# Value products of two attentions: one head's 64 columns per matmul, both heads in one PSUM bank

## The chip, the cores and the metric

The kernel runs on one core of a Trainium2 chip. TensorE multiplies; VectorE (DVE), ScalarE (ACT) and GpSimd (POOL) work element by element; SyncE (SP) issues most loads. The metric is the device time of one execution in microseconds. Before the change three runs took 876.66, 878.46 and 881.11 us; the median is 878.46.

## What is computed

Two attentions over 4 batches x 8 heads, 576 positions, head width 64, are added, and two MLPs follow on 2304 tokens of width 512:

```python
q_d, k_d, v_d = (a.reshape(B, H, 144, 4, D).mean(axis=3) for a in (q, k, v))   # pooled by 4
out_up = np.repeat(softmax(q_d @ k_d.T / 8) @ v_d, 4, axis=2)
mask = np.abs(pos[:, None] - pos[None, :]) < 4
out_local = softmax(np.where(mask, q @ k.T / 8, -1e9)) @ v
x = tokens(out_up + out_local)                                                  # 2304 x 512
x = np.maximum(np.maximum(x @ w1, x @ w2), x @ w3) @ w_out                      # 512 -> 768 -> 512
return np.maximum(0.01 * (h := x @ w_in), h) @ w_out2                           # 512 -> 2048 -> 512
```

## The kernel before

The tokens are cut into eight units of 288 (half a batch each), and the heads into four pairs; a pair's 2 x 64 values fill 128 rows of a tile.

The local attention of units 0 to 2 runs on TensorE, in steps named by letters: `pl_C` the scores in blocks of 96 queries by 102 keys (64 rows per head, line 399), `pl_D`, `pl_E`, `pl_H` and `pl_I` the softmax, `pl_O` the transposes (line 454), `pl_o` their two copies to `plt` (line 464; the first brings blocks 0 and 1, the second block 2), `pl_P` the value product (line 474), `pl_Q` the sum with the pooled output into `x32` (line 489), `pl_R` and `pl_S` the split of x into a high and a low part. Units 3 to 7 have their local attention as elementwise work on the other engines, called the lanes here: `local_load`, `qk_mult` on GpSimd, `qk_reduce` on VectorE and ScalarE, `pv_mult` and `pv_sum` on VectorE (lines 254 to 308).

The pooled attention of all four batches runs on TensorE: `ds_B` scores (line 548), `ds_M` transposes, `ds_N` the value product over two blocks of 72 keys (line 622), `ds_v` the copy of its output to `up` (lines 635 and 637).

In `pl_P` and `ds_N` before the change the weights are the values of both heads of the pair, 128 columns. Each head's attention is streamed through them, so each product holds 128 rows of which 64 are its head's own; the other 64 are not read. The two heads stand in two PSUM banks (`pl_P`) or in two column ranges of one bank (`ds_N`).

The first MLP layer is line 717 (18 groups of 12 matmuls a unit), its second layer line 747; the second MLP is lines 796 and 820.

Three things set the order. In the start, `ORDER` lists the steps of unit 0 and batch 0 by hand for all engines, with `fill` matmuls (line 169) in between. After it only SP's order is that of the code; for the other engines a scheduler orders the instructions by its own estimates of what is ready when. In both parts every engine works through its list in order. PSUM after the start is split into pools: `mm` with four banks for lines 717, 747 and 474, `at` with two for the pooled attention and transposes, `early` with two for scores.

Of the kernel before, what the change touches and what calls it, by code (L numbers as in the profile page):

```python
# [13 lines left out]
AF = mybir.ActivationFunctionType  # L14
ALU = mybir.AluOpType
# [5 lines left out]
FAC = 4  # L21
SD = S // FAC
# [7 lines left out]
NCOL = G * RU  # L30
# [5 lines left out]
QC = SD // 2  # L36
SCALE = 1.0 / 8.0
MASKED = -8.0e9
QB = 96
KB = QB + 2 * (FAC - 1)  # L40
NBLK = RU * G // QB
# [30 lines left out]
def local_global_attention_moe_kernel(  # L72
# [15 lines left out]
    V, A, P, T = nc.vector, nc.scalar, nc.gpsimd, nc.tensor  # L88
# [19 lines left out]
    for half in range(2):  # L108
        mk = const.tile([128, RC, WIN], F32, name=f"mask{half}")
        P.memset(mk, 0.0)  # L110
        for a in range(4):
            s = mk[32 * a : 32 * a + 32]
            if half == 0:
                P.affine_select(
                    out=s, in_=s, pattern=[[1, RC], [1, WIN]], base=-(FAC - 1),
                    channel_multiplier=1000, compare_op=ALU.is_ge, fill=MASKED,
                )
            else:
                P.affine_select(
                    out=s, in_=s, pattern=[[-1, RC], [-1, WIN]],  # L120
# [21 lines left out]
    for u in range(2):  # L142
# [5 lines left out]
        for j0, n, step, cm, base in conds:  # L148
            P.affine_select(
                out=bd[:, j0 : j0 + n], in_=bd[:, j0 : j0 + n], pattern=[[0, n], [step, KB]], base=base,  # L150
# [4 lines left out]
    def scratch(first, kind, name):  # L155
        if first == 0:
            tag = "l3" if name == "wl3" else "b"
            return PS["0"].tile([128, 512], F32, tag=tag, bufs=6 if tag == "b" else 1, name=name)
        return PS[kind].tile([128, 512], F32, tag=kind, name=name)
# [7 lines left out]
    def fill(what, t, n=None):  # L167
        for _ in range(FILL[what] if n is None else n):
            T.matmul(out=t, lhsT=warm[:, :128], rhs=warm, start=True, stop=True)
# [180 lines left out]
    pl = {}  # L350
# [107 lines left out]
    def pl_o(u, h):  # L458
# [5 lines left out]
            V.tensor_copy(out=t[:, j0:j1], in_=pt)  # L464
        pl[u, h, "aT"] = t

    def pl_P(u, h):
        t = pl.pop((u, h, "aT"))
        ps = pl[u, h, "o"] = [scratch(u, "mm", "ps_lo") for hh in range(2)]
        if u == 0:  # L470
            fill("P", ps[0])
        for hh in range(2):
            for j in range(NBLK):
                T.matmul(  # L474
                    out=ps[hh][:, j * QB : j * QB + QB], lhsT=pl[u // 2, h, "v"][:KB, u % 2, j], rhs=t[:, j, hh],
                    start=True, stop=True,
                )

    def pl_Q(u, h):
        ps = pl.pop((u, h, "o"))  # L480
        if h == 0:
            X[u] = (
                mmp.tile([128, 4, NCOL], F32R, tag="xh", bufs=2, name="xh"),
                mmp.tile([128, 4, NCOL], F32R, tag="xl", bufs=2, name="xl"),
            )
        x32 = pl[u, h, "x32"] = pools[u // 2].tile([128, NCOL], F32, tag="x32", bufs=2, name="x32")
        for hh in range(2):
            rows = slice(64 * hh, 64 * hh + 64)
            V.tensor_tensor(  # L489
                out=x32[rows].rearrange("p (s f) -> p s f", f=FAC),  # L490
                in0=ps[hh][rows, :NCOL].rearrange("p (s f) -> p s f", f=FAC),
                in1=up[u // 2][rows, h, u % 2 * QC : u % 2 * QC + QC].unsqueeze(2).to_broadcast((64, QC, FAC)), op=ALU.add,
            )

    def pl_R(u, h):
        A.activation(out=X[u][0][:, h], in_=pl[u, h, "x32"], func=AF.Copy)
# [7 lines left out]
    up = {}  # L504
    dst = {}
# [109 lines left out]
    def ds_N(b, h):  # L615
        ps = scratch(b, "at", "ps_up")
        if b == 0:
            fill("N", ps)
        ps = dst[b, h, "up"] = ps[:, : 2 * SD].rearrange("p (h s) -> p h s", h=2)
        for hh in range(2):  # L620
            for kc in range(2):
                T.matmul(  # L622
                    out=ps[:, hh], lhsT=dst[b, h, "v"][:, kc].rearrange("p h d -> p (h d)"),
                    rhs=dst[b, h, "aT", kc][:, 2 * hh : 2 * hh + 2].rearrange("p j s -> p (j s)"),
                    start=kc == 0, stop=kc == 1,
                )

    def ds_v(b, h):
        ps = dst.pop((b, h, "up"))
        if h == 0:  # L630
            up[b] = mmp.tile([128, 4, SD], F32, tag="up", bufs=2, name="up")
        for hh in range(2):
            rows = slice(64 * hh, 64 * hh + 64)
            if b == hh == 0:
                V.tensor_copy(out=up[b][rows, h, :], in_=ps[rows, hh])
            else:
                A.activation(out=up[b][rows, h, :], in_=ps[rows, hh], func=AF.Copy)

    def ds_stages(b, h):
        return [  # L640
            lambda: ds_load(b, h, "qk"),
            lambda: ds_pool_qk(b, h),
            lambda: ds_load(b, h, "v"),
            lambda: ds_pool_v(b, h),
            lambda: [f(b, h) for f in (ds_B, ds_F, ds_G, ds_J)],
            lambda: ds_norm(b, h),
            lambda: [f(b, h) for f in (ds_M, ds_m)],
            lambda: [f(b, h) for f in (ds_N, ds_v)],
        ]
# [59 lines left out]
    def L1_mm(u, m, e):  # L709
        xh, xl = X[u]  # L710
        ps = PS['mm'].tile([128, NCOL], F32, tag="mm", name="ps_h")
        terms = ((0, xh), (0, xl), (1, xh))
        order = [(wi, xx, kk) for wi, xx in terms for kk in range(KC)]
        if u == 0:
            order = [(wi, xx, kk) for kk in range(KC) for wi, xx in terms]
        for n, (wi, xx, kk) in enumerate(order):
            T.matmul(  # L717
                out=ps, lhsT=wA[m, e][wi][:, kk * 128 : kk * 128 + 128], rhs=xx[:, kk] if u < PEU else xx[:, :, kk, :],
                start=n == 0, stop=n == 3 * KC - 1
            )  # L720
        return ps
# [124 lines left out]
    with tc.manual_schedule(engines={ET.SP, ET.PE, ET.DVE, ET.Activation, ET.Pool}):  # L846
        nl = len(W1) - len(late)
        for what in "a0 a1 p0 a2 s0 p1 a3 s1 w0 p2 w1 s2 p3 w2 s3".split():
            if what[0] == "w":
                load_w1(W1[int(what[1])])  # L850
            else:
                pl_load(what[0], 0, int(what[1]))
        for t in W1[3:nl]:
            load_w1(t)
        steps = {
            "A": ds_pool_qk, "B": ds_B, "F": ds_F, "G": ds_G, "J": ds_J, "K": ds_norm, "M": ds_M, "m": ds_m,
            "N": ds_N, "v": ds_v, "C": pl_C, "D": pl_D, "E": pl_E, "H": pl_H, "I": pl_I, "O": pl_O, "o": pl_o,
            "P": pl_P, "Q": pl_Q, "R": pl_R, "S": pl_S,
        }
        fill("", scratch(0, "", "warm_ps"), FILL0)  # L860
        for w in ORDER.split():
            n = int(w[1])
            if w[0] in "xyzu":
                conv_step(W1[n])
            elif w[0] == "L":
                pl_pool_v(n)
            else:
                if w == "O0":
                    fill("", scratch(0, "", "warm_ps"), FILL1)
                steps[w[0]](0, n)  # L870
        ci = 8
        PS.pop("0").release()
        PS["mm"] = p1.enter_context(tc.tile_pool(name="ps_mm", bufs=4, space=PSUM, reuse_waits="tile"))
        PS["at"] = p1.enter_context(tc.tile_pool(name="ps_at", bufs=2, space=PSUM, reuse_waits="tile"))
        PS["early"] = tc.alloc_tile_pool(name="ps_early", bufs=2, space=PSUM, reuse_waits="tile")

    with tc.manual_schedule(engines={ET.SP}):
# [9 lines left out]
        for h in range(4):  # L887
            at(3 * h + 1, lambda h=h: [f(1, h) for f in (pl_C, pl_D, pl_E, pl_H, pl_I)])
            at(3 if h < 2 else B1[h - 2] + 2, lambda h=h: pl_load("a", 1, h))
            at(3 * h + 5, lambda h=h: [f(1, h) for f in (pl_O, pl_o)])  # L890
            at(3 * h + 6, lambda h=h: [f(1, h) for f in (pl_P, pl_Q, pl_R, pl_S)])
            at(4 if h < 2 else B1[h - 2] + 8, lambda h=h: pl_load("s", 1, h))
        for h in range(4):
            for w, fs in {
                "A": lambda h: ds_pool_qk(1, h),
                "v": lambda h: ds_load(1, h, "v"),
                "C": lambda h: [f(2, h) for f in (pl_C, pl_D, pl_E, pl_H, pl_I)],
                "B": lambda h: [f(1, h) for f in (ds_B, ds_F, ds_G, ds_J, ds_norm)],
                "L": lambda h: ds_pool_v(1, h),
                "O": lambda h: [f(2, h) for f in (pl_O, pl_o)],  # L900
                "M": lambda h: [f(1, h) for f in (ds_M, ds_m)],
                "P": lambda h: pl_P(2, h),
                "N": lambda h: [f(1, h) for f in (ds_N, ds_v)],
                "Q": lambda h: [f(2, h) for f in (pl_Q, pl_R, pl_S)],
            }.items():
                at(B1[h] + B1OFF[w], lambda h=h, fs=fs: fs(h))
# [18 lines left out]
        for u in range(NU):  # L925
# [10 lines left out]
            for s in range(PU):  # L936
# [17 lines left out]
                if s < NS:  # L954
                    m, e = divmod(s, 3)
                    ps = L1_mm(u, m, e)
# [7 lines left out]
                f = min(1, (s + 1) / NS)  # L964
# [87 lines left out]
```

## Time and profile before

| | |
|---|---|
| median of three runs | 878.46 us |
| the profiled execution | 879.78 us, of which the span from first to last instruction is 878.0 us |
| busy share of the span | TensorE 95%, VectorE 54%, ScalarE 47%, GpSimd 30% |
| granted TensorE clock, mean | 0.971 of full speed |
| chain that ended last | TensorE 75%, DMA 8%, VectorE 5%, ScalarE 4%, GpSimd 4% |

The start ends near 50 us. Units 0 to 2 fill the time to about 178 us, units 3 to 7 that to 470 us, and the second MLP the rest. Busy shares are averages over stages with different limits, so a stage is read by its own stretch. A matmul of f32 operands shows as two records on TensorE, each with its own weight load (PEld). A clock of 1.00 is 2.4 GHz, 0.50 is 1.2 GHz.

### The profile page before, as it was taken

What the parts mean: (1) busy time and instruction counts of PE and PEld (TensorE: products, weight loads), DVE (VectorE), ACT (ScalarE), POOL (GpSimd) and SP (SyncE); (2) the same over time, 40 slices, a digit from 0 to 9 for tenths busy, and PEclk for the clock granted to TensorE, in tenths of its full rate; (3) what the DMA queues carried; (4) which work ended last, traced back from release to release, by engine and by line L of the source; (5) the groups of instructions that cost most, each with busy time, mean ns of one, the idle gap of its engine ahead of it and who ended that gap; (6) DMA issues with size and microseconds to landing.
All of it is one profiled execution on the core that took longest, in us unless ns stands there. A gap on an engine that the chain in (4) does not pass through costs nothing.

```text
span 878.0 us, 13769 instructions
## 1 busy us (share of the span) xinstructions
PE 833.8 (95%) x5009; PEld 734.0 (84%) x5009; DVE 471.9 (54%) x912; ACT 413.4 (47%) x1556; POOL 260.1 (30%) x240
## 2 busy tenths in 40 slices
PE   8989997799999798999999999999999999999995
PEld 4778886799999698999998888888888888788894
DVE  6778758767767887422764995332233222322221
ACT  5788686536476585221654884322223222322221
POOL 6757796379658891101020000000000000000000
PEclk8989998699999899999999999999999999999998
DMA  9681422305233330130316800200021001100100
GB/s 279 247 341 26 164 80 70 112 24 171 99 108 110 120 97 28 29 128 6 107 77 242 360 1 1 84 13 1 1 64 33 1 1 36 36 1 1 29 20 24
DMA packets 27342, 73.98 MB, mean 84 GB/s; under 512 B 3082, under 2 KB 8138, under 8 KB 27274
## 3 DMA queue, kind: packets, MB, share of 16 engines
q1 hardware_dynamic: 22666, 68.38, 22.6%
q10 hardware_dynamic: 4608, 4.72, 1.5%
q8 instruction: 39, 0.64, 0.3%
q14 instruction: 29, 0.24, 0.1%
HBM read 63.65 MB, written 9.44 MB: 83 GB/s over the span
## 4 chain that ended last, share of the span: by engine, by line
PE 75%; DMA 8%; DVE 5%; ACT 4%; POOL 4%; issue 2%; SPq 1%; ACTq 0%; DVEq 0%; POOLq 0%
PE acc L820 22%; PE ps_g L796 22%; PE ps_h L717 19%; PE ps_o L747 6%; POOL qkprod L254 3%; DMA lk<-in_kL_dram 2%; ACT qkprod L267 2%; DMA dsrawv<-in_vP_dram 2%; PE ps_lo L474 1%; DMA raw<-x2d 1%; DMA wO<-in_w_out_dram 1%; PE ps_up L622 1%; DMA sv<-in_vW_dram 1%; PE ps_sc L548 1%; PE ps_ls L399 1%
## 5 line engine op out<-in xcount | busy, mean ns | idle before, releaser
L717 PE MATMUL ps_h<-xh,wA 128*128 128x288 f32 x1152 | 204.5, 307 | 10.6 <-DVE x L489 4.7
L717 PEld LDWEIGHTS ps_h<-xh,wA 128*128 128x128 f32 x1152 | 173.5, 195 | 15.8 <-DVE x L489 5.0
L820 PE MATMUL acc<-w2o,gh 128*128 128x512 f32 x576 | 178.0, 391 | 0.8 <-ACT gh L807 0.8
L796 PE MATMUL ps_g<-x2h,w2i 128*128 128x512 f32 (+1 forms) x640 | 158.9, 370 | 0.0
L804 DVE TENSOR_TENSOR g<-g,ps_g 128x512 f32<-128x512 f32 (+1 forms) x80 | 50.7, 634 | 189.0 <-ACT g L803 188.9
L803 ACT ACTIVATE g<-ps_g 128x512 f32<-128x512 f32 (+1 forms) x80 | 44.3, 553 | 190.2 <-PE ps_g L796 190.1
L796 PEld LDWEIGHTS ps_g<-x2h,w2i 128*128 128x128 f32 x640 | 114.6, 188 | 22.9
L820 PEld LDWEIGHTS acc<-w2o,gh 128*128 128x128 f32 x576 | 106.9, 188 | 23.2 <-ACT gh L807 1.2
L717 PE MATMUL ps_h<-xl,wA 128*128 128x288 f32 x576 | 113.2, 303 | 0.5 <-POOL xl L499 0.5
L820 PE MATMUL acc<-w2o,gl 128*128 128x512 f32 x288 | 112.1, 391 | 0.0
L254 POOL TENSOR_TENSOR qkprod<-lq,lk 128x1344 f32<-128x1344 f32 x30 | 91.8, 3072 | 8.6 <-DVE O L308 4.9
L717 PEld LDWEIGHTS ps_h<-xl,wA 128*128 128x128 f32 x576 | 91.3, 195 | 1.0 <-POOL xl L499 0.7
L267 ACT ACTIVATE qkprod<-qkprod 128x64 f32<-128x64 f32 x350 | 84.4, 248 | 14.4 <-POOL qkprod L254 14.3
L796 PE MATMUL ps_g<-x2l,w2i 128*128 128x512 f32 (+1 forms) x320 | 79.6, 370 | 0.0
L734 DVE TENSOR_TENSOR hm<-hm,ps_h 128x288 f32<-128x288 f32 x96 | 43.0, 448 | 67.3 <-PE ps_h L717 64.3
L747 PE MATMUL ps_o<-hh,wO 128*128 128x288 f32 x384 | 76.8, 297 | 0.0
L738 POOL TENSOR_TENSOR hl<-hm,hh 128x288 fp32r<-128x288 f32 x48 | 40.5, 846 | 116.9 <-ACT hh L737 116.9
L808 DVE TENSOR_TENSOR gl<-g,gh 128x512 fp32r<-128x512 f32 (+1 forms) x80 | 51.0, 637 | 39.6 <-ACT gh L807 35.1
L267 ACT ACTIVATION_READ_ACCUMULATOR qkprod<-qkprod 128x1 f32 x350 | 67.8, 194 | 0.0
L807 ACT ACTIVATE gh<-g 128x512 fp32r<-128x512 f32 (+1 forms) x80 | 47.0, 588 | 42.5 <-DVE g L804 42.1
L796 PEld LDWEIGHTS ps_g<-x2l,w2i 128*128 128x128 f32 x320 | 56.8, 188 | 10.9
L820 PEld LDWEIGHTS acc<-w2o,gl 128*128 128x128 f32 x288 | 54.1, 188 | 12.2 <-DVE gl L808 0.4
(131 smaller groups left out, 1157.8 us busy)
## 6 DMA issues: line engine op xcount, KB each, us to landing
wA<-in_wa_dram SPq DMA_DIRECT2D x18, 512.0 KB, 10.7
w2i<-in_w_in_dram SPq DMA_DIRECT2D x16, 512.0 KB, 7.5
w2o<-in_w_out_dram SPq DMA_DIRECT2D x16, 512.0 KB, 8.7
dsrawv<-in_vP_dram SPq DMA_DIRECT2D x16, 320.0 KB, 8.5
lk<-in_kL_dram SPq DMA_DIRECT2D x10, 480.0 KB, 6.9
lv<-in_vL_dram SPq DMA_DIRECT2D x10, 480.0 KB, 4.0
sqk<-in_qk_dram SPq DMA_DIRECT2D x8, 579.0 KB
dsraw<-in_qk_dram SPq DMA_DIRECT2D x8, 579.0 KB, 4.5
```

Source lines behind the costliest of these rows:

```text
L254: P.tensor_tensor(out=pr, in0=in0, in1=in1, op=ALU.mult)
L267: A.activation(out=pr[:, r, j], in_=pr[:, r, j], func=AF.Copy, accum_out=sc[:, r, j : j + 1])
L717: T.matmul(out=ps, lhsT=wA[m, e][wi][:, kk * 128 : kk * 128 + 128], rhs=xx[:, kk] if u < PEU else xx[:, :, kk, :], start=n == 0, stop=n == ...
L734: V.tensor_tensor(out=t, in0=t, in1=ps, op=ALU.max)
L738: P.tensor_tensor(out=hl[:, m], in0=t, in1=hh[:, m].bitcast(F32), op=ALU.subtract)
L747: T.matmul(out=ps, lhsT=wO[m][wi][:, os_], rhs=xx[:, m], start=n == 0, stop=n == 3 * M1 - 1)
L796: T.matmul(out=ps, lhsT=w2i[m][wi][:, kk * 128 : kk * 128 + 128], rhs=xx[:, kk, :n], start=j == 0, stop=j == 3 * KC - 1,)
L803: A.activation(out=g, in_=ps, func=AF.Copy, scale=0.01)
L804: V.tensor_tensor(out=g, in0=g, in1=ps, op=ALU.max)
L807: A.activation(out=gh, in_=g, func=AF.Copy)
L808: V.tensor_tensor(out=gl, in0=g, in1=gh.bitcast(F32), op=ALU.subtract)
L820: T.matmul(out=accs[c, t], lhsT=a[:, ts], rhs=w, start=m == 0 and j == 0, stop=m == M2 - 1 and j == 2)
```

## The change

Each matmul takes as weights only its own head's 64 columns and writes 64 rows of one bank: head 0 rows 0 to 63, head 1 rows 64 to 127. The loops run over blocks outside and heads inside. The sum of `pl_Q` and the copy of `ds_v` become one instruction of 128 rows; for batch 0 the copy's first half was VectorE's and is ScalarE's now.

```diff
     def pl_P(u, h):
         t = pl.pop((u, h, "aT"))
-        ps = pl[u, h, "o"] = [scratch(u, "mm", "ps_lo") for hh in range(2)]
+        ps = pl[u, h, "o"] = scratch(u, "mm", "ps_lo")
         if u == 0:
-            fill("P", ps[0])
-        for hh in range(2):
-            for j in range(NBLK):
+            fill("P", ps)
+        for j in range(NBLK):
+            for hh in range(2):
+                rows = slice(64 * hh, 64 * hh + 64)
                 T.matmul(
-                    out=ps[hh][:, j * QB : j * QB + QB], lhsT=pl[u // 2, h, "v"][:KB, u % 2, j], rhs=t[:, j, hh],
+                    out=ps[rows, j * QB : j * QB + QB], lhsT=pl[u // 2, h, "v"][:KB, u % 2, j, rows], rhs=t[:, j, hh],
                     start=True, stop=True,
                 )
...
-        for hh in range(2):
-            rows = slice(64 * hh, 64 * hh + 64)
-            V.tensor_tensor(
-                out=x32[rows].rearrange("p (s f) -> p s f", f=FAC),
-                in0=ps[hh][rows, :NCOL].rearrange("p (s f) -> p s f", f=FAC),
-                in1=up[u // 2][rows, h, u % 2 * QC : u % 2 * QC + QC].unsqueeze(2).to_broadcast((64, QC, FAC)), op=ALU.add,
-            )
+        V.tensor_tensor(
+            out=x32.rearrange("p (s f) -> p s f", f=FAC), in0=ps[:, :NCOL].rearrange("p (s f) -> p s f", f=FAC),
+            in1=up[u // 2][:, h, u % 2 * QC : u % 2 * QC + QC].unsqueeze(2).to_broadcast((128, QC, FAC)), op=ALU.add,
+        )
...
-        ps = dst[b, h, "up"] = ps[:, : 2 * SD].rearrange("p (h s) -> p h s", h=2)
-        for hh in range(2):
-            for kc in range(2):
+        dst[b, h, "up"] = ps
+        for kc in range(2):
+            for hh in range(2):
                 T.matmul(
-                    out=ps[:, hh], lhsT=dst[b, h, "v"][:, kc].rearrange("p h d -> p (h d)"),
+                    out=ps[64 * hh : 64 * hh + 64, :SD], lhsT=dst[b, h, "v"][:, kc, hh],
                     rhs=dst[b, h, "aT", kc][:, 2 * hh : 2 * hh + 2].rearrange("p j s -> p (j s)"),
                     start=kc == 0, stop=kc == 1,
                 )
...
-        for hh in range(2):
-            rows = slice(64 * hh, 64 * hh + 64)
-            if b == hh == 0:
-                V.tensor_copy(out=up[b][rows, h, :], in_=ps[rows, hh])
-            else:
-                A.activation(out=up[b][rows, h, :], in_=ps[rows, hh], func=AF.Copy)
+        A.activation(out=up[b][:, h, :], in_=ps[:, :SD], func=AF.Copy)
```

The scheduler's order changes with it, and line numbers after line 488 shift by up to six (717 becomes 711, 622 becomes 621, 474 becomes 476). Counted over TensorE's whole order, the shape in which the array is used (whole, row halves, column halves) changes 93 times before and 144 times after.

TensorE at the first value product of unit 1, before:

```order
L454 MATMUL ps_lt<-ident,ple 102x96 x6
L391 LDWEIGHTS ident_b
L391 MATMUL ps_ls<-band_122,ident_b 96x306
L399 MATMUL ps_ls<-sqk 96x102 x3
L474 MATMUL ps_lo<-plt,sv 128x96 x6
L717 MATMUL ps_h<-xh,wA_0_697 128x288
```

And the same value product after:

```order
L476 MATMUL ps_lo<-plt,sv 64x96 x4
L711 MATMUL ps_h<-xh,wA_0_686 128x288
L711 MATMUL ps_h<-xl,wA_0_686 128x288
L711 MATMUL ps_h<-xh,wA_0_686 128x288 x2
L711 MATMUL ps_h<-xl,wA_0_686 128x288
L711 MATMUL ps_h<-xh,wA_0_686 128x288 x2
L711 MATMUL ps_h<-xl,wA_0_686 128x288
L711 MATMUL ps_h<-xh,wA_0_686 128x288 x2
L711 MATMUL ps_h<-xl,wA_0_686 128x288
L711 MATMUL ps_h<-xh,wA_0_686 128x288
L476 MATMUL ps_lo<-plt,sv 64x96 x2
L711 MATMUL ps_h<-xh,wA_1_708 128x288
```

The six matmuls were one block behind scores; now four and two stand apart, with nine rows (twelve matmuls) of the MLP between them.

VectorE at the end of the start, before (`up` is the pooled output, `wl` and `wy` are weight conversions):

```order
L193 SCALAR_TENSOR_TENSOR wy<-wy,wl_626 128x512
L489 TENSOR_TENSOR x_663<-ps_lo,up 64x288 x2
L464 COPY plt<-ps_lt 102x384
L464 COPY plt<-ps_lt 102x192
L190 SCALAR_TENSOR_TENSOR wl_667<-wA_0_174,wl_667 128x512
L193 SCALAR_TENSOR_TENSOR wy<-wy,wl_667 128x512
L635 COPY up<-ps_up 64x144
L489 TENSOR_TENSOR x_703<-ps_lo,up 64x288 x2
```

And after:

```order
L193 SCALAR_TENSOR_TENSOR wy<-wy,wl_619 128x512
L489 TENSOR_TENSOR x_655<-ps_lo,up 128x288
L464 COPY plt<-ps_lt 102x384
L464 COPY plt<-ps_lt 102x192
L190 SCALAR_TENSOR_TENSOR wl_658<-wA_0_174,wl_658 128x512
L193 SCALAR_TENSOR_TENSOR wy<-wy,wl_658 128x512
L489 TENSOR_TENSOR x_692<-ps_lo,up 128x288
```

The copy to `up` has left, and each of the two sums is one row of 128 partitions instead of two of 64.

VectorE at a value product of unit 2, between work of the lanes (`lp`, `pvprod`, `O`), before:

```order
L464 COPY plt<-ps_lt 102x384
L290 RECIPROCAL lsm<-lp 128x9
L464 COPY plt<-ps_lt 102x192
L734 TENSOR_TENSOR hm<-hm,ps_h 128x288
L291 TENSOR_TENSOR lp<-lp,lsm 128x63
L301 TENSOR_TENSOR pvprod<-lp,lv 128x1344 x2
L438 TENSOR_SCALAR ps_ls<-plsm 96x3
L562 TENSOR_REDUCE ps_sc<-ps_sc 72x2
L438 TENSOR_SCALAR ps_ls<-plsm 96x3
L308 TENSOR_REDUCE O<-pvprod 128x3x64
L489 TENSOR_TENSOR x_1925<-ps_lo,up 64x288 x2
```

And after:

```order
L464 COPY plt<-ps_lt 102x384
L301 TENSOR_TENSOR pvprod<-lp,lv 128x1344
L464 COPY plt<-ps_lt 102x192
L301 TENSOR_TENSOR pvprod<-lp,lv 128x1344
L438 TENSOR_SCALAR ps_ls<-plsm 96x3
L308 TENSOR_REDUCE O<-pvprod 128x3x64
L438 TENSOR_SCALAR ps_ls<-plsm 96x3
L489 TENSOR_TENSOR x_1900<-ps_lo,up 128x288
```

The second copy to `plt` moved behind the first `pvprod`; the sum stands behind the first reduction to `O` in both.

## Rows read from the trace of the kernel before

**Rows 1.** Page: busy us, share of the span and instructions of each engine
```profile
PE 833.8 (95%) x5009; PEld 734.0 (84%) x5009; DVE 471.9 (54%) x912; ACT 413.4 (47%) x1556; POOL 260.1 (30%) x240
```

**Rows 2.** Busy us (instructions) of each engine by stretch, TensorE clock, DMA
```profile
core 0: us, PE busy (x) PEld busy (x) DVE busy (x) ACT busy (x) POOL busy (x), PEclk, DMA share, GB/s
25.00:50.00 25.00, 21.58 (x176) 17.03 (x174) 20.60 (x62) 18.51 (x58) 16.37 (x16) 1.00 0.56 221
50.00:78.00 28.00, 24.77 (x168) 22.02 (x169) 22.07 (x53) 23.59 (x67) 18.41 (x17) 0.88 0.67 249
78.00:112.00 34.00, 33.91 (x252) 30.17 (x251) 26.14 (x78) 25.47 (x87) 25.95 (x22) 1.00 0.31 107
...
150.00:176.00 26.00, 18.64 (x107) 18.05 (x106) 20.07 (x32) 14.22 (x91) 12.31 (x10) 0.71 0.32 109
...
229.00:260.00 31.00, 31.00 (x240) 30.06 (x238) 21.70 (x50) 17.67 (x100) 18.32 (x15) 1.00 0.34 116
260.00:300.00 40.00, 34.00 (x254) 32.69 (x254) 33.57 (x53) 25.86 (x169) 32.27 (x26) 0.91 0.41 144
```

**Rows 3.** Timeline of TensorE and its weight loads: start, us, records, [idle before]
```profile
78.78 1.42 PEld L474 LDWEIGHTS ps_lo<-plt,sv 102*128 102x128 f32 x12 [0.26 <-DVE plt L464]
...
80.11 0.19 PEld L717 LDWEIGHTS ps_h<-xh,wA 128*128 128x128 f32 x1
...
97.11 0.52 PEld L474 LDWEIGHTS ps_lo<-plt,sv 102*128 102x128 f32 x4 [0.19 <-issue]
97.73 0.45 PEld L548 LDWEIGHTS ps_sc<-dsqk 64*72 64x72 f32 x4
98.36 0.97 PEld L474 LDWEIGHTS ps_lo<-plt,sv 102*128 102x128 f32 x8 [0.19 <-issue]
...
23.10 1.14 PE L622 MATMUL ps_up<-dsvaT 72*128 72x144 f32 x8
...
24.39 0.45 PEld L548 LDWEIGHTS ps_sc<-dsqke 64*72 64x72 f32 x8 [0.33 <-issue]
25.04 0.11 PEld L169 LDWEIGHTS <-warm 128*128 128x128 bf16 x2 [0.19 <-DVE plt L464]
```

**Rows 4.** Groups by line and form: count | busy us, mean ns | idle before
```profile
L734 DVE TENSOR_TENSOR hm<-hm,ps_h 128x288 f32<-128x288 f32 x96 | 43.0, 448 | 67.3 <-PE ps_h L717 64.3 <-ACT hm L731 2.3
...
L489 DVE TENSOR_TENSOR x<-ps_lo,up 64x288 f32<-64x288 f32 x24 | 10.8, 451 | 1.0 <-ACT up L637 0.5
...
L637 ACT ACTIVATE up<-ps_up 64x144 f32<-64x144 f32 x28 | 8.0, 285 | 19.2 <-PE ps_up L622 14.1 <-DVE up L635 4.9
...
L622 PE MATMUL ps_up<-dsvaT 72*128 72x144 f32 x32 | 4.6, 285 | 0.0
```

**Rows 5.** Chain of waits in the start: start, us, what
```profile
30.91 0.98 PE ps_up L622 x8
...
32.33 1.31 PE ps_lo L474 x12
...
40.30 0.22 DVE up L635
```

**Rows 6.** SP queue: waits (us, times, longest), and issues by time
```profile
SPq L359 <- PE ps_ls L399: 27.2, 2, 23.6
...
91.67 0.35 SPq L359 DMA_DIRECT2D sqk<-in_qk_dram  x1
92.06 0.44 SPq L243 DMA_DIRECT2D lq<-in_qL_dram  x1
```

**Rows 7.** Timeline: the two matmul rows that begin after TensorE's long waits
```profile
146.57 1.33 PE L717 MATMUL ps_h<-xh,wA 128*128 128x288 f32 x4 [4.74 <-DVE x L489]
...
164.16 2.29 PE L622 MATMUL ps_up<-aT,dsv 72*128 72x144 f32 x8 [3.67 <-DVE plt L464]
```

**Rows 8.** TensorE busy us (instructions) and granted clock in two stretches
```profile
145.00:150.00 5.00, 3.43 (x14) 0.50 0.00 0
...
165.00:170.00 5.00, 5.00 (x28) 0.50 0.00 0
```

## The prediction

> **What bounds the kernel now.** I read the page's shares first, then the busy time by stretch, then the chain of waits, and then single matmuls. TensorE is busy for 95% of the span [rows 1], and from 78 to 112 us and again from 229 to 260 us it never rests, at full clock [rows 2]. Before 78 us it rests 3.4 us of 25 and 3.2 of 28; in 150 to 176 and 260 to 300 us it rests 7.4 and 6.0 us [rows 2]. So matmul time counts in full in the busy stretches, and elsewhere only where TensorE is what the others wait for. From 383 us on nothing of the change runs; the second MLP merely starts earlier or later. Call the value product of a unit's head pair P (pl_P, 12 calls, 4 of them in the hand-ordered start) and that of the pooled attention N (ds_N, 16 calls, 4 in the start).
>
> **What a call costs today.** An f32 product appears as two records. P's twelve start at 78.78 and the next line's first weight load at 80.11 [rows 3]: 1.33 us, 0.111 each, for only 96 streamed columns. N's eight take 1.14 us with a last one of 0.285 [rows 3, 4], so (1.14 - 0.285) / 7 = 0.122 each for 144 columns. The score product L548 streams the same 144 columns, on halves of the array: eight records, two halves alternating, begin at 24.39 and the next line at 25.04 (0.65 us); four records on one half take from 97.73 to 98.36 (0.63 us) [rows 3]. Hence two halves in turn cost what one costs: they run side by side. The four need 4 x 0.122 = 0.49, so entering or leaving the halves adds 0.14. Four P records between two such blocks last from 97.11 to 97.73, 0.62 instead of 4 x 0.111 = 0.45: 0.17. I price a change of the array's shape at 0.16 us.
>
> **The matmuls after it.** As many, with 64 weight columns instead of 128, the two heads on the two column halves. No row shows column halves; the nearest are L548's row halves. If they behave alike, a pair takes its matmul time: N 0.122, P 0.122 x 96/144 = 0.081. P becomes 6 x 0.081 = 0.49 (0.84 less), N 4 x 0.122 = 0.49 (0.49 less); 12 x 0.84 + 16 x 0.49 = 17.9 us. If they do not run side by side, P takes 12 x 0.081 = 0.97 and N stays: 4.3 us less. I take the first, as L548 is the nearest row. Against it stand shape changes. Counted over the whole order of TensorE they rise from 93 to 144, because P and N used to share the full array's shape with the MLP, and because the scheduler now often cuts P into four and two matmuls with MLP matmuls between. 51 x 0.16 = 8.2 us. Net 9.7 us, by place: start 5.3 - 16 x 0.16 = 2.7; unit 1's P 3.4 - 7 x 0.16 = 2.2; unit 2's P with the four N of batch 1, 5.3 - 11 x 0.16 = 3.5; the eight later N 3.9 - 17 x 0.16 = 1.2.
>
> One rule of the Trainium skill speaks against this. L548's eight records show weight loads hidden behind matmuls on the same rows, since their 0.122 is matmul alone; L474 shows it for the full array. "TensorE: Matmul & The Clock Gate", Part 3, "The mechanism", says that a weight load overlaps running matmuls only where the row group differs, and here both heads stand on the same rows. The same page's "Measured speedup vs the span model" lists three column tiles at 2.38 times one, which is for the pairing. The trace contradicts the first for the full array and shows nothing for column halves; what it would cost is the last rival.
>
> **The other engines.** The sum with the pooled output becomes one VectorE instruction of 128 rows in place of two of 64. 64 rows take 0.451, 128 rows of the same length 0.448 (L734) [rows 4]: 12 x 0.45 = 5.4 us less. The copy of N becomes one ScalarE instruction. A half takes 0.285 there [rows 4]; the whole lies between that and 0.57, both halves one after the other, and I take 0.285, since rows did not matter on VectorE. VectorE loses four copies of 0.22 in the start [rows 5], ScalarE 12 x 0.285 = 3.4 later. P holds one of the pool's four banks instead of two.
>
> **What of it lies on the path.**
> - *Start.* The chain passes N (0.98), P (1.31) and the VectorE copy (0.22) [rows 5]. By name: 0.98 - 0.49 - 0.32 = 0.17, 1.31 - 0.49 - 0.32 = 0.50, and 0.22: 0.9 us. At most it is VectorE's whole 4 x (0.45 + 0.22) = 2.7. VectorE is busy 20.6 of 25 us there, ScalarE 18.5 [rows 2], and they wait for each other; I take 2.0. Late next: weight conversions between ScalarE and VectorE.
> - *Unit 1.* TensorE is full, so 2.2, less a little for the P that lies before 78 us: 1.9. It is not lost afterwards, because the SP queue stands behind the scores: the load at 91.67 waits up to 23.6 us for L399, and the first loads of the lanes (lq) are issued right behind it at 92.06 [rows 6]. Earlier scores start the lanes earlier. Bounds 0.3 (no pairing) to 2.2.
> - *Unit 2.* TensorE waits for VectorE anyway: 4.74 us for x (line 489), which holds banks that the next MLP matmuls need, and 3.67 for plt [rows 7]. In VectorE's order both stand behind work of the lanes and behind earlier sums, so four sums less give up to 1.8, and the free bank lets 12 MLP matmuls go into the first wait. The 3.5 of matmul mostly turn into rest. I take 1.5, bounds 0 and 4.7.
> - *Later N.* 1.2 in a full stretch; 0.8, bounds -2.7 (no pairing, same shape changes) and 1.2.
>
> Sum 6.2. From 260 to 300 us the lanes set the pace and TensorE rests 6.0 [rows 2]; I let 1.1 be lost there: 5.1. The profiled execution took 879.78 (span 878.0 and 1.8 around it), 1.3 above the median of the runs, 878.46. It would become 874.7; against the median, **873.4 us**. Own range of this case 868.5 to 877.
>
> **Rivals.**
> - *The clock gives back more.* It stood at 0.50 in 145 to 150 us with 3.43 busy, and in 165 to 170 with 5.00 [rows 8], after those two waits. At full speed 1.7 and 2.5 are saved; with shorter waits I add 4: 869. For it: the free bank shortens the wait for x. Against: plt still stands behind lane work.
> - *Absorbed.* Lanes and loads set the pace up to 383 us, and only the named 0.9 of the start and some 0.8 arrive: 876.8. For it: the rests in 150 to 176 and 260 to 300. Against: the lanes' loads wait for TensorE.
> - *No pairing.* P still gives 0.36 a call, N nothing. Start 4 x 0.36 - 2.6 = 1.2 longer on TensorE against VectorE's 2.0: 0.8 gained; unit 1 4 x 0.36 - 1.1 = 0.3 gained; unit 2 1.0 from VectorE; later 2.7 lost: together 0.6 longer, 879.
> - *Slower: rest turns into half clock.* Place: 150 to 176 us, where the clock is 0.71 and TensorE is busy 18.64 [rows 2]. With 3.5 us fewer matmuls between the same waits, it may not recover between them. All at 0.50, the work takes 18.64 x 0.71 / 0.50 = 26.5, 7.8 longer; with the 2.0 and 1.9 from before it 882.4, and with the 0.8 and lane starts lost too some 885. It decides from where the clock there falls under 0.6. Against: the freed bank and the four sums shorten the waits.
> - *Weight loads not hidden (the page's rule).* A load of 64 columns, half of 0.111, stands before each matmul: P 12 x (0.055 + 0.081) = 1.63, N 8 x 0.177 = 1.42, so 0.30 and 0.44 longer a call, with the shape changes 20 us of TensorE. On the path: unit 1 4 x 0.30 + 1.1 = 2.3, the later N 8 x 0.44 + 2.7 = 6.2, the start 4 x 0.74 + 2.6 less VectorE's 2.0 = 3.6: 12.1, so 890.5.
>
> **How the numbers follow.** Forecast 0.52, clock gives back 0.11, absorbed 0.10, no pairing 0.09, half clock 0.13, loads not hidden 0.05. Half a per cent, about what a measurement can tell from no change, is 4.4 us: 874.1 and 882.9. Two thirds of the forecast's chance lies below 874.1 (0.36), with the returned clock 0.47 for faster. Slower is 0.10 of the half clock, the 0.05, and 0.02 of no pairing: 0.17. The rest, 0.36, is within. The range takes in the near end of the half clock and most of the returned one, and leaves out the rule's 890, the far end of the half clock and a tail below: 866.5 to 883.
>
> **What would show it.** Right: P's records in pairs a few ns apart, six pairs in about 0.5 us, N's four pairs in 0.5; 0.16 at each end; the first lq load near 88 instead of 92.06; L489 at 0.45 for 128 rows; from 383 on the same matmuls about 5 us earlier. Wrong: single records 0.08 (P) and 0.12 (N) apart; 0.14 and 0.18 for the rule; shape changes well over 0.16; or the clock in the stretch after 150 us far from 0.71, which would move the time by more than all terms together.

## The result, and the profile after

The changed kernel takes 870.25 us, the median of 4 runs (869.22 to 872.17). The kernel before took 878.75 beside it, also 4 runs (876.66 to 881.11). The ratio is 0.9905, with a 95% interval of 0.9882 to 0.9929. So the change saves 8.5 us, where 5.1 were forecast (873.4, range 866.5 to 883). Direction and range held. The experiments below show that the 8.5 hangs on more than the terms of the forecast.

The page's line of shares, which answers to [rows 1]; the profiled execution took 870.67, its span 868.8:

```profile
PE 820.8 (94%) x5005; PEld 712.4 (82%) x5009; DVE 464.0 (53%) x896; ACT 409.2 (47%) x1544; POOL 263.9 (30%) x240
```

TensorE is busy 13.0 us less, VectorE 7.9 less, and the span is 9.2 shorter. So TensorE rests 48.0 us instead of 44.2.

The groups by line and form, answering to [rows 4] (P is L476 now, N L621, the sum still L489, N's copy L631):

```profile
L476 PE MATMUL ps_lo<-plt,sv 102*64 102x96 f32 x144 | 10.8, 268 | 2.5 <-DVE plt L464 2.5
L621 PE MATMUL ps_up<-aT,dsv 72*64 72x144 f32 x96 | 9.8, 321 | 6.7 <-DVE plt L464 5.2 <-DVE lp L288 1.5
...
L489 DVE TENSOR_TENSOR x<-ps_lo,up 128x288 f32<-128x288 f32 x12 | 5.4, 450 | 4.2 <-PE ps_lo L476 2.2 <-ACT up L631 2.0
L631 ACT ACTIVATE up<-ps_up 128x144 f32<-128x144 f32 x16 | 4.6, 288 | 12.2 <-PE ps_up L621 12.2
L621 PE MATMUL ps_up<-dsvaT 72*64 72x144 f32 x32 | 2.8, 299 | 0.0
```

The same view of the kernel before has, beside N's 4.6 in [rows 4]:

```profile
L474 PE MATMUL ps_lo<-plt,sv 102*128 102x96 f32 x144 | 20.8, 291 | 0.4 <-DVE plt L464 0.3
...
L622 PE MATMUL ps_up<-aT,dsv 72*128 72x144 f32 x96 | 16.1, 308 | 4.6 <-DVE plt L464 4.6
```

P's busy time was 20.8, and N's 16.1 + 4.6. They are now 10.8 and 12.6. The sum takes 0.450 for 128 rows and the copy 0.288, each as long as a half took before.

TensorE and its weight loads in the start, answering to [rows 3] (start, us, records, idle before):

```profile
23.64 0.44 PEld L621 LDWEIGHTS ps_up<-dsvaT 72*64 72x64 f32 x8 [0.42 <-issue]
...
24.28 0.10 PEld L169 LDWEIGHTS <-warm 128*128 128x128 bf16 x1 [0.20 <-issue]
...
25.78 0.53 PEld L476 LDWEIGHTS ps_lo<-plt,sv 102*64 102x64 f32 x12 [0.42 <-DVE plsm L439]
...
26.43 0.11 PEld L169 LDWEIGHTS <-warm 128*128 128x128 bf16 x2
```

From N's first load to the next line's first load it is 0.64 us, and from P's 0.65. Both were priced at 0.49 and a change of shape of 0.16. The single records show the pairs: P's twelve begin at 25.786 and 25.792, 25.919 and 25.926, 26.002 and 26.008, and so on. Two lie 6 or 7 ns apart, and the pairs 0.082, but for the first, after which 0.133 pass. That interval and the one to the next line together show one change of shape. The other, on entering, shows where P stands between MLP matmuls:

```profile
74.96 0.19 PEld L711 LDWEIGHTS ps_h<-xh,wA 128*128 128x128 f32 x1
...
75.31 0.36 PEld L476 LDWEIGHTS ps_lo<-plt,sv 102*64 102x64 f32 x8 [0.17 <-DVE plnm L414]
...
75.79 0.19 PEld L711 LDWEIGHTS ps_h<-xh,wA 128*128 128x128 f32 x1
```

From the MLP's load at 74.96 to P's first it is 0.35, where two loads of the MLP in a row begin 0.13 apart: entering costs 0.22. (It is 0.35 at 13 such places of P and N, whatever releaser the row names.) From P's first to the next line it is 0.48 for four pairs of 0.082: 0.15 more.

The stretches of [rows 2], moved earlier by up to 8 us for the lead (columns as there):

```profile
25.00:48.00 23.00, 18.83 (x177) 11.45 (x176) 18.05 (x55) 18.30 (x58) 16.71 (x16) 1.00 0.64 249
48.00:74.00 26.00, 21.07 (x155) 18.56 (x156) 20.41 (x48) 22.78 (x60) 18.59 (x18) 0.87 0.67 257
74.00:108.00 34.00, 33.48 (x267) 28.79 (x265) 25.53 (x79) 25.63 (x92) 25.34 (x22) 1.00 0.31 107
143.00:169.00 26.00, 15.13 (x96) 13.30 (x95) 21.27 (x38) 13.61 (x89) 14.88 (x11) 0.63 0.30 108
221.00:253.00 32.00, 32.00 (x248) 30.86 (x247) 21.93 (x54) 17.63 (x100) 19.55 (x17) 1.00 0.34 115
253.00:292.00 39.00, 31.94 (x231) 29.17 (x230) 31.27 (x52) 26.21 (x175) 32.80 (x29) 0.87 0.43 152
```

TensorE rests more in each stretch that already had rests: 10.9 us of 26 after 143 (7.4 of 26 before), 7.1 of 39 after 253 (6.0 of 40). The granted clock reads 0.63 there instead of 0.71, and 0.87 instead of 0.91. These stretches do not hold the same work (96 matmul records after 143, where [rows 2] have 107 after 150), so they tell little of the clock; the next section cuts at equal work.

TensorE's longest waits, answering to [rows 7] (us in all, times, longest), and the first load of the lanes on the SP queue, answering to [rows 6]:

```profile
PE ps_up L621 <- DVE plt L464: 5.2, 3, 4.4
PE ps_aT L599 <- DVE dssum L583: 4.1, 1, 4.1
...
PE ps_h L711 <- DVE x L489: 3.4, 1, 3.4
```

```profile
89.34 0.43 SPq L243 DMA_DIRECT2D lq<-in_qL_dram  x1
```

TensorE still waits for VectorE's plt and x. The lanes (the unpooled attention, two of them for each unit from 3 on) begin 2.7 us earlier.

### The profile page after: what moved, and what is told of

Read it like the earlier page. It is cut to its first block, busy times and chain, and to the rows that moved or that the text cites. A ratio compares the mean times of both kernels' runs of the same rounds, so it can differ in the third digit from the quotient of the medians.

```text
span 868.8 us, 13727 instructions
## 1 busy us (share of the span) xinstructions
PE 820.8 (94%) x5005; PEld 712.4 (82%) x5009; DVE 464.0 (53%) x896; ACT 409.2 (47%) x1544; POOL 263.9 (30%) x240
## 4 chain that ended last, share of the span: by engine, by line
PE 74%; ACT 2%; DMA 1%; SPq 0%; DVE 0%; issue 0%; ACTq 0%
PE acc L814 22%; PE ps_g L790 22%; PE ps_h L711 20%; PE ps_o L741 7%; DMA raw<-x2d 1%; PE ps_sc L547 1%; ACT qkprod L267 1%; PE ps_up L621 1%; PE ps_aT L599 0%; PE ps_x L663 0%; SPq L832 0%; ACT dse L572 0%; DVE ob L822 0%; ACT ev L744 0%; ACT xh L698 0%
## 5 line engine op out<-in xcount | busy, mean ns | idle before, releaser
L254 POOL TENSOR_TENSOR qkprod<-lq,lk 128x1344 f32<-128x1344 f32 x30 | 91.9, 3073 | 4.5 <-DMA lk<-in_kL_dram 3.4
L790 PEld LDWEIGHTS ps_g<-x2l,w2i 128*128 128x128 f32 x320 | 56.8, 188 | 10.9
```

The lines of the kernel that those rows point to most:

```text
L254: P.tensor_tensor(out=pr, in0=in0, in1=in1, op=ALU.mult)
L790: T.matmul(out=ps, lhsT=w2i[m][wi][:, kk * 128 : kk * 128 + 128], rhs=xx[:, kk, :n], start=j == 0, stop=j == 3 * KC - 1,)
```

## Where the lead arises

I cut the two executions at the same work: the last matmul of unit 0's first MLP product (105.4 us before, 101.6 now), the first of unit 2's (198.3 and 190.7), the first of unit 6's (391.8 and 382.8). From there on the distance no longer changes. The two middle pieces of the kernel before (columns as in [rows 2]):

```profile
105.40:198.30 92.90, 79.72 (x560) 74.79 (x558) 64.62 (x121) 55.21 (x354) 65.19 (x46) 0.89 0.23 73
198.30:391.80 193.50, 184.09 (x1372) 178.33 (x1373) 132.91 (x252) 106.24 (x629) 112.77 (x99) 0.97 0.29 97
```

and of the changed kernel:

```profile
101.60:190.70 89.10, 73.53 (x559) 66.24 (x558) 63.04 (x117) 53.81 (x350) 69.56 (x47) 0.89 0.23 76
190.70:382.80 192.10, 184.41 (x1372) 175.63 (x1373) 131.28 (x251) 103.97 (x621) 112.73 (x99) 0.96 0.29 98
```

The lead is 3.8 us at unit 0's end, 3.8 more by unit 2 and 1.4 more after it. In the first piece TensorE has 6.2 us less to do, of which 3.8 arrive and the rest is waiting. The granted clock of this piece is 0.89 in both kernels.

## The experiments

Theory A: TensorE's time in the full stretches pays. B: the shorter work of VectorE and ScalarE pays. C: the free bank pays. Theories D to J came as the runs called for them, and their texts say what they are. The times are medians beside the kernel before on the same chip; before was 878.33, 878.93 and 878.40 in the three groups of runs.

**p_only**: the diff's edits to pl_P and pl_Q alone.

> Only the change's P half on the kernel before: P on column halves in one bank with one sum of 128 rows; N and its copies as before. 13 shape changes more (106 instead of 93). Theory A (TensorE's time in the full stretches pays, and the rests in unit 2 get shorter): P 10 us less of matmul, 13 x 0.16 = 2.1 more; most of the path's gain is P's: the chain to the lane loads about 3 us earlier, unit 2's stretch 3 more, time 872 to 874.5. Theory B (the gain comes from the shorter work of VectorE and ScalarE, and of that most from the four VectorE copies of N at the start): under half of the gain here, 875 to 877. Theory C (the free bank of the matmul pool is what pays): nearly the whole gain, 870 to 871.5.

881.65 us, ratio 1.0041 (1.0024 to 1.0058): slower than before. None of the three theories has this.

**n_only**: the diff's edits to ds_N and ds_v alone.

> Only the change's N half on the kernel before: N on column halves with one copy of 128 rows; P in two banks and with two sums as before. 20 shape changes more (113). Theory A: N 7.8 us less of matmul, 20 x 0.16 = 3.2 more, some 2.5 of it on the path (start 1, unit 2 and later 1.5): 875.5 to 877. Theory B (the copies of N decide): 872 to 874.5. Theory C (the bank decides): no gain to speak of, 877.5 to 879.

874.80 us, ratio 0.9961 (0.9942 to 0.9979): between A's 875.5 and B's 874.5. The two halves give +3.3 and -3.5, together about nothing, and the whole gives -8.5. What decides is not a sum over parts.

**te_only**: the changed kernel with the sum and the copy in two halves again.

```diff
-        V.tensor_tensor(
-            out=x32.rearrange("p (s f) -> p s f", f=FAC), in0=ps[:, :NCOL].rearrange("p (s f) -> p s f", f=FAC),
...
+        for hh in range(2):
+            rows = slice(64 * hh, 64 * hh + 64)
+            V.tensor_tensor(
+                out=x32[rows].rearrange("p (s f) -> p s f", f=FAC),
+                in0=ps[rows, :NCOL].rearrange("p (s f) -> p s f", f=FAC),
...
-        A.activation(out=up[b][:, h, :], in_=ps[:, :SD], func=AF.Copy)
+        for hh in range(2):
+            rows = slice(64 * hh, 64 * hh + 64)
+            if b == hh == 0:
+                V.tensor_copy(out=up[b][rows, h, :], in_=ps[rows, :SD])
+            else:
+                A.activation(out=up[b][rows, h, :], in_=ps[rows, :SD], func=AF.Copy)
```

> The changed kernel with the sum (line 489 of before) as two instructions of 64 rows again, and N's copy as two again, the first one on VectorE: TensorE's work and the one bank stay as changed, the VectorE and ScalarE parts are undone. 139 shape changes. Theory A: 5.4 us come back on VectorE and 3 on ScalarE, of which the start feels about 1.5 and unit 2 about 1.5: 872 to 874. Theory B: nearly all of the gain is gone, 876 to 879. Theory C: nearly nothing lost, 870 to 871.5.

879.05 us, ratio 1.0012 (0.9997 to 1.0027). It looks like B, but p_only, which has the merged sum, gains nothing either.

**no_alt**: `for hh in range(2)` outside, `for j` and `for kc` inside, in pl_P and ds_N of the changed kernel.

> The changed kernel with the head's loop outside: the matmuls on column halves come three (P) and two (N) of one half in a row instead of in turn. Everything else, 144 shape changes too, as changed. If two halves in turn is what makes them run side by side, P takes 10 x 0.081 or so, 0.3 to 0.5 more a call, and N 2 to 4 x 0.122, 0.25 to 0.49 more a call: 8 to 14 us more of TensorE. Theory A: 4 to 8 of it arrive at the end, 874 to 878. Theories B and C: most of the gain stays, 870.5 to 873.

880.14 us, ratio 1.0008 (0.9991 to 1.0025), over all that was expected. It is 10 us slower than the changed kernel, with only 5.9 more of TensorE's busy time. The array did not do what I expected, either. The weight loads of P and of an N in the start of no_alt:

```profile
24.59 0.74 PEld L476 LDWEIGHTS ps_lo<-plt,sv 102*64 102x64 f32 x12 [0.42 <-DVE plt L464]
...
41.78 0.45 PEld L621 LDWEIGHTS ps_up<-dsvaT 72*64 72x64 f32 x8 [0.42 <-issue]
42.43 0.11 PEld L169 LDWEIGHTS <-warm 128*128 128x128 bf16 x2 [0.20 <-issue]
```

N takes 0.65 to the next line, as when the halves alternate. In the records the second head's first matmul starts 13 ns after the first head's first, though three other records stand between them in the program. (The records do not name the head; their spacing tells it, 13 ns within a pair and 0.122 from pair to pair.) P's second head starts 0.22 us after its first and runs beside it: the next line's load begins at 25.45, 0.86 after P's first, against 0.65. So the order of the halves was worth 0.2 for P and nothing for N there.

**What the four have in common.** The lead at unit 0's end is 3.8 in p_only, 2.5 in n_only, 4.7 in te_only, 1.4 in no_alt. It is lost, or not, after that. A good mark is when the seventh of the lanes' 30 sums (line 308) begins, 191.43 us in before: 7.6 earlier in the changed kernel, 4.6 in n_only, 1.2 in te_only, 0.4 in p_only and 0.3 in no_alt. That is the order of their medians but for p_only and no_alt, which change places; the last three lie 0.7 to 3.3 us over before. Unit 3's input is transposed from the lanes' output, and the first matmul of unit 3's MLP comes 8.1 earlier than in before in the changed kernel, 5.7 in n_only, 1.7 in te_only, and 1.1 and 1.2 later in p_only and no_alt. VectorE in p_only shows a kind of wait that makes work late (start, us, what):

```profile
129.49 0.22 DVE L288 TENSOR_REDUCE lp<-lp 128x9 f32<-128x63 f32 x1
129.74 4.70 DVE L289 TENSOR_SCALAR lp<-lp 128x9 f32<-128x9 f32 x1
134.48 0.22 DVE L290 RECIPROCAL lsm<-lp 128x9 f32<-128x9 f32 x1
134.73 0.98 DVE L291 TENSOR_TENSOR lp<-lp,lsm 128x63 f32<-128x63 f32 x1
135.64 0.54 DVE L464 COPY plt<-ps_lt 102x384 f32<-102x384 f32 x1
```

Line 289 adds a constant to 9 numbers a row. Elsewhere that takes 0.17 us; here it takes 4.70, and the copy to plt stands behind it. TensorE waits for that plt, 5.29 us at 136.24. GpSimd in the same stretch:

```profile
128.87 1.14 POOL L587 TENSOR_TENSOR dse<-dse,dssum 72x576 f32<-72x576 f32 x1
129.97 0.72 POOL L519 TENSOR_TENSOR dsv<-dsrawv 72x256 f32<-72x256 f32 x1
130.66 0.78 POOL L736 TENSOR_TENSOR hl<-hm,hh 128x288 fp32r<-128x288 f32 x1
131.41 3.01 POOL L254 TENSOR_TENSOR qkprod<-lq,lk 128x1344 f32<-128x1344 f32 x1
```

GpSimd goes from one instruction straight to the next, and line 289 ends at 134.44, when line 254 ends (134.42). Why it ends there is open, since GpSimd's next, line 518, follows as closely (134.38). In te_only the product L301, 1.55 us elsewhere, takes 7.30 from 145.87 on, beside GpSimd's L254, L501, L443 and L740, which run without a gap from 146.00 to 151.75; 1.42 later it is done. The Trainium skill's "SBUF — State Buffer", section "SBUF: two separate sides", has a rule for it: VectorE and GpSimd share one pair of ports as a lock, which a VectorE instruction in a two-port mode or with two SBUF inputs needs. The trace agrees that the one stands while the other runs; it stood through four of GpSimd's instructions, where the page speaks of one. It goes the other way too: in te_only GpSimd's line 254 at 140.60 takes 4.57 instead of 3.07. Over 0.5 us more than usual, GpSimd's instructions after the start add up to 2.1 in before, 5.6 in the changed kernel, 2.5 in n_only, 3.2 in p_only, 4.8 in te_only and 4.5 in no_alt.

The wait shown is not the one in which p_only's lanes fall back. After it their first three sums still begin 5.3 to 6.1 us earlier than in before. The fourth is 3.3 earlier, after line 291 has taken 3.85 instead of 0.23 (at 155.20). The sixth is only 0.2 earlier, after line 301 has taken 3.56 instead of 1.55 (at 182.64) and line 254 behind it 4.42 (at 184.74).

Over lines 281, 289, 291 and 301, all on the first two lanes' score rows in SBUF, I add up what lies over the line's median wherever that is more than 0.6 us, from 110 to 200 us: 5.9 in before, 7.5 in the changed kernel, 5.0 in n_only, and 10.9 in p_only, 13.0 in te_only, 11.3 in no_alt. (The 7.1 and 14.1 in the expectations below are too high by 1.2 and 3.2.) All later lanes have these rows in PSUM, and the four lines have no such excess after 200 us. So the next four move the rows of the first two lanes to PSUM as well:

```
         if i // 2 == PEU:
-            pb = pools["att"].tile([128, n + 2 * RU], F32, tag="lp", bufs=2, name="lp")
+            pb = PS["mm"].tile([128, NCOL], F32, tag="mm", name="lp")[:, : n + 2 * RU]
```

**p_only_lp**

> p_only, with the score rows of the first two lanes (lp of line 276) in a bank of the matmul pool instead of in SBUF, as all later lanes have theirs in PSUM. Theory D (p_only loses in unit 2 what it gains before, because VectorE's instructions on those rows, L281, L289, L291 and L301, stand still while GpSimd is busy; instructions over 0.6 us longer than their line's median add up to 14.1 us from 110 to 200 us in p_only, 7.1 in before, 7.5 in the changed kernel): the excess falls under 2 us, unit 3 begins 5 us or more earlier than in before instead of 1.1 later, 870 to 874. Theory E (the order of the instructions that came out anew decides, the standing still only goes with it): no such relation, 876 to 883. Theory F (the matmul pool is short of banks in unit 2, and giving one away for 20 us hurts): 882 or more.

871.55 us, ratio 0.9921 (0.9905 to 0.9937), 10 less than p_only. The excess on the four lines is gone, GpSimd's with it, and unit 3's first MLP matmul comes 7.8 us earlier than in before. All this is as D had it. The edit also gives VectorE a new order from 126 us on, so the order is not excluded as a part of the 10.

**te_only_lp**

> te_only, with the score rows of the first two lanes in a bank of the matmul pool. Theory D: the 13.0 us by which VectorE's instructions are too long from 110 to 200 us fall under 2, time 869 to 873 instead of 879. Theory E: 875 to 882. Theory F: over 880.

875.45 us, ratio 0.9962 (0.9942 to 0.9982). No excess is left, but the time is 2.5 above D's range and within E's: D gave back 3.6 of the 8.8 us that te_only lies over the changed kernel.

**after_lp**

> The changed kernel, with the score rows of the first two lanes in a bank of the matmul pool. Theory D: its 7.5 us of excess go too, half of it on the path: 864 to 868. Theory E: anything from 866 to 880. Theory F: 872 or more.

870.78 us, ratio 0.9911 (0.9896 to 0.9927): no gain, though the 7.5 us are gone. D fails here, and E, which allowed 866 to 880, is not tested by it.

**before_lp**

> The kernel before, with the score rows of the first two lanes in a bank of the matmul pool; its P holds two of the pool's four banks. Theory D: its 7.1 us of excess go, half of it on the path: 873 to 876, and against it the changed kernel with the same edit is 6 to 10 us faster. Theory E: anything from 872 to 884. Theory F: it hurts most here, 880 or more.

869.75 us, ratio 0.9901 (0.9885 to 0.9917): better than D's range, and as fast as the changed kernel without its change. With the rows in PSUM the change is worth nothing: 0.9911 against 0.9901, intervals that overlap. D had expected the changed kernel to be 6 to 10 us faster here, so this half of it fails. F falls in all four, since no time reaches its bounds.

No excess is left in any of the four, on VectorE or on GpSimd. What they gain does not follow what they lost by it: 10.9 us of excess went with a gain of 10.1 (p_only), 13.0 with 3.6 (te_only), 7.5 with none (the changed kernel) and 5.9 with 9.2 (before). So the waits are shown, and that the edit removes them; how much of a gain is theirs and how much the new order's is not.

Where does it go? before_lp after unit 0, as cut above:

```profile
107.70:193.50 85.80, 78.21 (x568) 72.68 (x566) 55.55 (x125) 54.91 (x355) 65.25 (x52) 0.94 0.30 99
193.50:383.60 190.10, 181.95 (x1364) 176.53 (x1365) 134.33 (x247) 106.19 (x629) 110.96 (x93) 0.98 0.27 90
```

and after_lp:

```profile
101.60:187.30 85.70, 75.86 (x559) 67.67 (x557) 53.34 (x120) 53.18 (x344) 64.29 (x52) 0.90 0.27 86
187.30:381.60 194.30, 184.13 (x1373) 175.07 (x1374) 134.62 (x247) 103.64 (x627) 112.61 (x94) 0.96 0.28 94
```

The first piece now takes the same 85.8 and 85.7, at the lower clock (0.90) where TensorE has less to do; the second takes 4.2 us more. Of after_lp's lead of 6.1 us at unit 0's end, 4.1 melt away by unit 6: from 110 to 390 us TensorE rests 20.0 us in it and 15.7 in before_lp. (Of the runs, the profiled one of after_lp is the fastest and that of before_lp the slowest, so up to 2.8 us of the lead may be chance.) Theory G says that the lanes set that pace. The last four test it: on top of the rows in PSUM they leave out part of the lanes' work. The products of line 254 run over 32 of 64 columns, and those of line 301 over 3 of 7 window places; the sums are cut likewise.

```
-        in0 = qt[:, c * RC : c * RC + RC, :].unsqueeze(2).to_broadcast((128, RC, WIN, D))
+        in0 = qt[:, c * RC : c * RC + RC, : D // 2].unsqueeze(2).to_broadcast((128, RC, WIN, D // 2))
...
-        in0 = p[:, c * RC : c * RC + RC, :].unsqueeze(2).to_broadcast((128, RC, D, WIN))
+        in0 = p[:, c * RC : c * RC + RC, :3].unsqueeze(2).to_broadcast((128, RC, D, 3))
```

**before_light**

> before_lp with the lanes' work cut, which leaves out part of the computation: the products of line 254 and their sums run over 32 of 64 columns, those of lines 301 and 308 over 3 of 7 window places. It is the measure for the next three. Theory G (from unit 1 on the lanes on GpSimd, VectorE and ScalarE set the pace, and TensorE's saved time turns into rest): TensorE's rests from 110 to 390 us, 15.7 us in before_lp, fall under 8, 850 to 860. Theory H (the lanes are not what TensorE waits for): 866 or more.

854.42 us (853.88 to 855.56), with 5.1 us of rest from 110 to 390:

```profile
110.00:200.00 90.00, 86.60 (x646) 81.87 (x645) 49.83 (x139) 63.69 (x454) 58.55 (x63) 0.96 0.34 111
200.00:300.00 100.00, 98.27 (x752) 94.43 (x751) 58.15 (x158) 63.55 (x424) 58.44 (x64) 1.00 0.35 117
300.00:390.00 90.00, 90.00 (x681) 88.71 (x680) 33.16 (x79) 26.91 (x101) 14.62 (x18) 1.00 0.14 46
```

G holds, and H (866 or more) falls: TensorE did wait for the lanes. In before_lp the busy times were 82.41, 93.39 and 88.47.

**after_light**

> The changed kernel with the score rows in a bank and the lanes' work cut in the same way. Theory G: now the change is worth most of its TensorE time, 6 to 10 us less than before_light (after_lp against before_lp gave 1.0 more). Theory J (the gain of the change on the kernel as it stands came from the order alone, and its TensorE time is eaten by shape changes): within 3 us of before_light.

848.87 us (848.61 to 852.25), 5.6 less than before_light, no run of the one within the other's range. The gain is 5.6, just under G's 6 to 10; its mechanism holds. J, within 3, falls.

**p_only_light**

> p_only with the score rows in a bank and the lanes' work cut in the same way. Theory G: P has over half of the net TensorE time, 4 to 7 us less than before_light, and between before_light and after_light. Theory J: within 3 us of before_light, on either side.

852.56 us (851.04 to 855.39), 1.9 less than before_light: between the two, as G had it, but smaller than its 4 to 7. By size alone it fits J, so this run does not tell the two apart.

**no_alt_light**

> no_alt with the score rows in a bank and the lanes' work cut in the same way. Theory G: the lost pairing (826.75 us of TensorE's work in no_alt, 820.81 in the changed kernel) arrives: 3 to 6 us more than after_light. Theory J: within 3 us of after_light, on either side.

853.64 us (852.76 to 854.97), 4.8 more than after_light, as G had it. Its TensorE is busy 820.5 us against 816.1.

## Why the prediction was right, point by point

- *P and N.* Right. The pairs run side by side on column halves, P at 0.082 and N at 0.122 a pair. P fell by 10.0 us of busy time (12 x 0.84 = 10.1 forecast) and N by 8.1 (16 x 0.49 = 7.8). The rivals *no pairing* and *loads not hidden* fall with that.
- *Changes of shape.* Near: 0.22 on entering and 0.15 on leaving, where 0.16 was forecast for each. By these, 51 more cost some 9.5 us instead of 8.2 (an estimate). TensorE's busy time even so fell by 13.0, where the net forecast was 9.7; no row shows what made up the 3.3.
- *VectorE and ScalarE.* Right: 0.450 for the sum over 128 rows (0.45), 0.288 for the copy (0.285). A copy that left VectorE took 0.286 and not 0.22, which is only the part of it that stands in the chain; the bound of 2.7 for the start should be 2.9.
- *Start.* 2.0 forecast; the first MLP matmul came 2.45 earlier. That is about as fine as one execution can tell: before_lp has the same instructions in the same order up to there and began it 1.2 later than before, and ended unit 0 2.3 later. The pieces below are no more certain than that.
- *Unit 1.* 1.9 forecast, up to unit 0's end 1.4 was seen (3.8 less 2.45). The lanes' first load was forecast near 88 and came at 89.34.
- *Unit 2.* This term was too small: 1.5 forecast, 3.8 measured from unit 0's end to unit 2. I had seen TensorE's waits for x and plt, had bounded the term by 0 and 4.7, and had put them down to lane work ahead in VectorE's order. I had not looked at how long that lane work takes. In the trace of before this line had stood, for 9 numbers a row:

```profile
158.24 3.30 DVE L289 TENSOR_SCALAR lp<-lp 128x9 f32<-128x9 f32 x1
```

p_only has the same lead at unit 0's end (3.8) and P's whole saving, though not N's, and took 93.1 us over this piece against before's 92.9. So P's saving alone does not bring the 3.8. VectorE's excess is 10.9 there, 5.9 in before and 7.5 in the changed kernel; that it makes the difference is likely and not shown.
- *The later N and the lanes.* 0.8 less 1.1 forecast, which is a loss of 0.3; 1.4 were gained. That the lanes set the pace from 260 to 300 us was right, and holds for more of the kernel than that: with the lanes light the change is worth 5.6 us, with the stalls gone and the lanes whole nothing.
- *Rests and the clock.* Part of the saved matmul time did turn into rest, 2.4 of the 6.2 us between unit 0's end and unit 2. The clock after 143 us reads 0.63, just above the 0.6 at which the rival *half clock* was to decide, but over equal work it is 0.89 as before. *The clock gives back more* came nearest with 869, for a reason that did not occur: the clock did not rise. *Absorbed* had the mechanism that before_lp and after_lp show.

So the forecast had the prices right, and the sum nearly, partly by luck. With the lanes' work cut the whole change is worth 5.6 us. On the kernel as it stands, versions with most of the saving came out anywhere from 3.3 us slower (p_only) to 8.5 faster, and each has an order of its own on VectorE, GpSimd and TensorE. The waits of VectorE and GpSimd for each other are the likely cause of p_only's loss, since taking them away, with a new order, gave 10 us back. For te_only they can be a part only, and no_alt was not run with the rows in PSUM alone. That before_lp, p_only_lp, after_lp and the changed kernel all lie within 869.7 to 871.6 fits with the lanes' pace, as the light kernels show it; which engine of the three that share the lanes is the narrowest stays open. No version that computes the whole was clearly faster than the changed kernel.

## What to carry to other kernels

A saving on the busiest engine is worth only what the stretches let through; run the same change once with the other engines' work cut, and once with its halves apart, before believing the whole. When a scheduler sets the order, every edit is also a new order: compare at the same piece of work, on each engine, and look for instructions that last many times their usual. A VectorE instruction that reads its operands from SBUF while GpSimd is busy is the first to look at; moving one tile of 81 columns (one for each of two lanes) to PSUM made the kernel before as fast as this whole change did.

## What the runs showed of the hardware

- Two column halves over the same rows run side by side with their weight loads hidden: 0.082 us a pair of records for 96 columns, 0.122 for 144, in pairs 6 or 7 ns apart.
- Going from the whole array to column halves cost 0.22 us between first loads, and going back 0.15.
- The two halves need not alternate in the program. In no_alt the second half's first matmul of N started 13 ns after the first's, past three others.
- VectorE can stand for 4 to 6 us over an instruction with operands in SBUF (0.17 us became 4.70, and 1.55 became 7.30) while GpSimd runs from one instruction into the next. GpSimd stands too (3.07 became 4.57). With the rows of two lanes in PSUM neither was seen.
